# Reordering the weight conversion and the products of the first two chunk indices in a linear-attention and feed-forward kernel

## The chip, the cores and the metric

The kernel runs on one core of one Trainium2 chip. The metric is device time in microseconds (us) of one execution. TensorE does matrix products (PE in the profile, its weight loads PEld), VectorE (DVE) and ScalarE (ACT) do elementwise work, GpSimd (POOL) only fills constants here, and SyncE (SP) issues all DMAs in one queue. Each engine takes its instructions in the order in which they were built and waits for semaphores at the head of its queue.

## The reference: what is computed

For 4 batches, 8 heads, 768 time steps and 48 channels a linear-attention recurrence is computed, and its output, laid out as 3072 tokens by 384, goes through a multiplicative feed-forward block:

```python
for t in range(S):
    cur = einsum('bhd,bhe->bhde', u * k[t], v[t])
    y[t] = einsum('bhd,bhde->bhe', r[t], state + cur)
    state = w * state + einsum('bhd,bhe->bhde', k[t], v[t])
x = y.transpose(0, 2, 1, 3).reshape(3072, 384)
out = ((x @ w1) * (x @ w2)) @ w3 @ w_out     # 384 -> 1024 -> 1024 -> 384
```

The arrays r, k, v, w and u are float32. The feed-forward weights come as float64, and the kernel turns them into float32 itself.

## The kernel before, in words

**Units.** Time is cut into 6 chunks of 128 steps (the chunk index c), and a unit n is one chunk of one batch b: n = 4c + b, 24 units in all. The recurrence runs from chunk to chunk through the state st of each batch. For a unit the kernel does, in the names of the code:

- `load` (line 129): three DMAs of 192 KB, k and r into krin (3 buffers) and v into vnat (3 buffers).
- `scale` (306): VectorE multiplies k and r by powers of w into krs (2 buffers), line 310.
- `diagonal` (314): VectorE forms r*k*u and its sums dg (lines 319 to 321), and ScalarE puts them on the diagonal of AT with eight activations (line 326).
- `turn` (337), for units 0 to 4: TensorE transposes k and r (line 342), and ScalarE copies them out (line 344) as kT and tt. From unit 5 on the transposition goes through VectorE (line 352), a DMA to a scratch in DRAM (354), four DMAs back (362) and a ScalarE copy (367).
- `pairs` (370): TensorE's k-v products (389) and r-k products (395) into PSUM; VectorE updates st (403, 408, 409); ScalarE spreads st into wide (420); VectorE puts the masked r-k products over the diagonal in AT (416).
- `output` (455): TensorE's products of the state (473) and of AT with v (483); ScalarE copies the sum into xT, the feed-forward input of the chunk (488).

**Feed-forward.** For each chunk index, x @ w1 and x @ w2 are made in 8 column blocks j of 128: `ab(c, j)` (line 493) computes three products of 128x512 into ps_a, a ScalarE copy (502), three into ps_b, and a VectorE multiplication (506) into abt. A block can be done for half of the tokens (batches 0 and 1, or 2 and 3): then the products have 256 columns. The profile counts every such float32 product as two matmuls. w3 and w_out are multiplied once into a 1024x384 matrix (`fold`, 290), and `sums` and `o` (524, 534) finish the output.

**Weights.** w1 and w2 are cut in strips of 256 columns: piece 2z is strip z of w1, piece 2z + 1 is strip z of w2, 8 pieces in all, 768 KB each. `fetch` (147) asks for the float64 words of a piece into one of three raw buffers. `convert` (254) makes float32 of them: ScalarE line 266, VectorE lines 267, 268 and 269, ScalarE line 271, VectorE line 272. Block j needs strip j // 2 of both matrices. Pieces 0 and 1 are fetched before the program branches (165, 170); a piece whose raw buffer is still in use waits on SyncE, and everything behind it in SyncE's queue waits too.

**Order of the work.** The order is written out by hand in `beside` (586): for every chunk index a list of 8 slots, two to a unit; the first is done ahead of the unit's output, the second behind the next unit's pairs. From index 2 on the slots are cut from one merged list. The loop (606 to 636) takes, for unit n: loads, scale, diagonal and turn of unit n + 1, slot 2b, output of n, pairs of n + 1, slot 2b + 1. The instruction streams that are built follow this order only roughly, since the tool that builds the program places instructions by its own priorities; where the text speaks of the built order, the streams of the finished programs were read.

Of the kernel before, what the change touches and what calls it, by code (L numbers as in the profile page):

```python
# [21 lines left out]
def kernel(  # L22
# [35 lines left out]
    B, H, S, D = r.shape  # L58
# [8 lines left out]
    DF = moe_w3.shape[0]  # L67
    KM = DM // P
    KF = DF // P
# [3 lines left out]
    STRIP = 256  # L73
# [7 lines left out]
    def rows(i):  # L81
        return slice(i * PAD, (i + 1) * PAD)
# [46 lines left out]
    def load(n, which="krv"):  # L129
        if n >= NU:  # L130
            return
        c, b = units[n]
        ts = slice(c * C, (c + 1) * C)
        for nm, src, dst in (("k", k, krin[n % NIN][:, 0]), ("r", r, krin[n % NIN][:, 1]), ("v", v, vnat[n % NV][:, :, :D])):
            if nm in which:
                nc.sync.dma_start(out=dst, in_=src[b, :, ts, :].rearrange("h t d -> t h d"))
# [10 lines left out]
    def fetch(piece):  # L147

        dst, src = piece
        if src.dtype != U64:  # L150
            nc.sync.dma_start(out=dst, in_=src)
            return None
        _, m, n = src.shape
        raw = raws[sent[0] % NRAW][:, :m * n].rearrange("p (m n) -> p m n", m=m)
        sent[0] += 1
        nc.sync.dma_start(out=raw, in_=src)
        return raw
# [25 lines left out]
    with tc.tile_pool(name="once", bufs=1) as once, tc.tile_pool(name="psW", bufs=2, space=PSUM) as psW:  # L183
# [12 lines left out]
        for l in range(LEVELS):  # L196
            n = 1 << l
# [20 lines left out]
    def body(arm, fast):  # L218
# [13 lines left out]
        else:  # L232
# [6 lines left out]
            for l in range(LEVELS):  # L239
                n = 1 << l  # L240
# [13 lines left out]
        def convert(piece, raw):  # L254
            dst, src = piece
            if src.dtype != U64:
                return
            _, m, n = src.shape
            lo, hi = (raw.bitcast(U32).rearrange("p m (n z) -> p m n z", z=2)[:, :, :, z] for z in range(2))
            t, power = (once.tile([P, RAW], F32, tag="cv", bufs=3 if fast else 2, name=nm)[:, :m * n].rearrange("p (m n) -> p m n", m=m)  # L260
                        for nm in ("t", "power"))
            tb, hb, pb = t.bitcast(U32), dst.bitcast(U32), power.bitcast(U32)

            nc.scalar.activation(out=power, in_=hi.bitcast(F32), func=ABS)  # L266
            nc.vector.tensor_scalar_max(power, power, 2.0 ** -15)  # L267
            nc.vector.tensor_scalar(tb, hi, 0x80000000, None, ALU.bitwise_and)
            nc.vector.scalar_tensor_tensor(hb, pb, 3, tb, ALU.logical_shift_left, ALU.bitwise_xor)  # L269

            nc.scalar.activation(out=t, in_=lo, func=IDENTITY, bias=two, scale=2.0 ** -51)  # L271
            nc.vector.tensor_add(hb, hb, tb)
# [33 lines left out]
        def scale(n):  # L306

            kr = krin[n % NIN]
            if fast:
                nc.vector.tensor_mul(krs[n % NS][:, :, :, :D], kr, pn[:, :, :, :D])  # L310
            else:
                nc.scalar.copy(out=krs[n % NS][:, :, :, :D], in_=kr)
# [142 lines left out]
        def output(n):  # L455
            c, b = units[n]
            rw = rT[n]
            if not fast:
                rw = work.tile([P, NP, C], F32, tag="kl", bufs=1, name=f"rw{n}")
                for p in range(NP):  # L460
                    nc.gpsimd.tensor_mul(rw[:, p].rearrange("x (a t) -> x a t", a=2),
                                         rT[n][:, p].rearrange("x (a t) -> x a t", a=2),
                                         pw[:, p, None, :].to_broadcast([P, 2, T]))
            yt = psY.tile([P, 2, 512], F32, tag="y", name=f"ps_y{n}")
            ps = yt[:, :, :KM * T].rearrange("x a (q t) -> x a q t", q=KM)


            blocks = [(p, j, divmod(3 * p + j, P // Q)) for p in range(NP) for j in range(3)]
            to = lambda a, q, g: ps[g * Q:(g + 1) * Q, a, q, :]
            held = range(0 if c else 1, 2)  # L470
            for a in held:
                for p, j, (q, g) in blocks:
                    nc.tensor.matmul(to(a, q, g), lhsT=wide[a][n % 2][:, p, j * Q:(j + 1) * Q], rhs=rw[:, p, 2 * a:2 * a + 2] if fast else rw[:, p, rows(a)],  # L473
                                     start=(q == 0), stop=False, skip_group_check=True)

            vv = vnat[n % NV].rearrange("t h d -> t (h d)")
            parts = [(h, f) for h in range(H) for f in range(h * D // PAD, ((h + 1) * D - 1) // PAD + 1)]
            seen = set()
            for h, f in sorted(parts, key=lambda e: (e[0] * D > e[1] * PAD, e[1])):
                x = h * PD + f * PAD - h * D  # L480
                q, g = divmod(f, 2)
                for a in range(2):
                    nc.tensor.matmul(ps[rows(g), a, q, :], lhsT=vv[rows(a), x:x + PAD], rhs=AT[n][rows(a), h % 2, h // 2, :],  # L483
                                     start=(a not in held and (a, g) not in seen), stop=True, skip_group_check=True)
                    seen.add((a, g))
            if b == 0:
                xT[c] = work.tile([P, KM, NT], F32, tag="xT", bufs=2, name=f"xT{c}")
            nc.scalar.copy(out=xT[c][:, :, b * C:(b + 1) * C].rearrange("x q (a t) -> x a q t", a=2), in_=ps)  # L488
# [70 lines left out]
        def AB(c, js=range(KF), ts=slice(0, NT)):  # L559
            return [lambda c=c, j=j: ab(c, j, ts) for j in js]  # L560

        def O(c):
            return [lambda c=c, j=j: sums(c, j) for j in range(KH)] + [lambda c=c, m=m: o(c, m) for m in range(B // 2)]

        def first(i):
            if i not in landed:
                landed[i] = fetch(ab_pieces[i])
            convert(ab_pieces[i], landed[i])

        W12 = [[lambda i=i: first(i) for i in (2 * z, 2 * z + 1)] for z in range(DF // STRIP)]  # L570
        WO = [lambda c=c: out_weight(c) for c in range(KF)]

        def W3(js):
            return [s for j in js for s in ([lambda j=j, z=z: w3_weight(j, z) for z in range(DF // PIECE)]
                                            + [lambda j=j: fold(j)])]

        def merge(*lists):

            keyed = [((i + 0.5) / len(x), m, s) for m, x in enumerate(lists) for i, s in enumerate(x)]
            return [s for _, _, s in sorted(keyed, key=lambda e: e[:2])]  # L580
# [3 lines left out]
        halves = [slice(0, NT // 2), slice(NT // 2, NT)]  # L584
        none = []
        beside = [
            [none, none, none, W12[0] + AB(0, range(0, 2), halves[0]), none, W12[1][:1], none,
             AB(0, range(0, 2), halves[1]) + W12[1][1:] + AB(0, range(2, 4))],
            [none, W12[2], none, AB(0, range(4, 6)), none, W12[3], none, AB(0, range(6, 8))],
            merge(AB(1), WO + W3(range(3))),  # L590
            merge(AB(2, range(1)), W3(range(3, KF))) + [sums_of_weights] + merge(AB(2, range(1, lead)), O(0)[:KH])
            + O(0)[KH:] + AB(2, range(lead, KF)),
            O(1) + merge(O(2), AB(3)),
# [4 lines left out]
        before = dict(landed)  # L598

        free = B + 1 if fast else NU + 1  # L600
        scale(0)
        diagonal(0)
        turn(0)
# [2 lines left out]
        for c in range(NCH):  # L606
            plan = beside[c]
            if not isinstance(plan[0], list):
                cuts = [len(plan) * m // (2 * B) for m in range(2 * B + 1)]
                plan = [plan[cuts[m]:cuts[m + 1]] for m in range(2 * B)]  # L610
            for b in range(B):
                n = c * B + b
                while asked <= (n + 3 if n + 3 >= free else n + 2):
                    load(asked, "kr")
                    asked += 1
                load(n + 2, "v")
                if n + 1 < min(NU, free):
                    scale(n + 1)
                if n + 1 < NU:
                    diagonal(n + 1)  # L620
                    if n + 1 >= free:
                        turn_rows(n + 1)
                if n + 1 < min(NU, free):
                    turn(n + 1)
                if free <= n + 2 < NU:
                    scale(n + 2)
                    turn_blocks(n + 2)
                for step in plan[2 * b]:
                    step()
                output(n)  # L630
                if free <= n + 2 < NU:
                    turn_places(n + 2)
                if n + 1 < NU:
                    pairs(n + 1)
                for step in plan[2 * b + 1]:
                    step()
        for step in tail:
            step()
        landed.clear()
# [38 lines left out]
```

## Time and profile before

| what | value |
|---|---|
| median of 5 runs | 526.21 us (525.19 to 526.72) |
| the profiled execution's own time | 527.77 us |
| its span, first to last instruction | 525.8 us |
| mean granted TensorE clock | 0.986 |
| TensorE busy | 496.1 us |
| VectorE busy | 281.5 us |
| ScalarE busy | 195.5 us |
| HBM read, written | 39.65 MB, 12.19 MB |
| TensorE busy in 20 to 40, 40 to 60 us | 17.62, 14.99 us |
| VectorE busy in 20 to 40, 40 to 60 us | 18.04, 18.97 us |
| TensorE busy in 300 to 400 us | 100.00 us |

How to read it: the page gives one profiled execution. Its slices are fortieths of the span, some 13.1 us each, with the busy share in tenths. In a timeline line the numbers are the start and the length, then engine, line of the code, operation, tiles, shapes and the count of instructions; in brackets stands the idle time ahead of the group and what ended it. Start to start, neighbouring instructions of one engine lie closer than their lengths, because they overlap at their ends.

### The profile page before, as it was taken

How to read it: one execution, taken by the hardware profiler on the slowest of the kernel's cores; microseconds unless marked ns; L12 is line 12 of the kernel's file. 1: busy time of each engine (PE TensorE's matmuls, PEld its weight loads, DVE VectorE, ACT ScalarE, POOL GpSimd, SP SyncE). 2: the span in 40 equal slices, each digit the busy share in tenths (PEclk: the TensorE clock that was granted, in tenths of full speed). 3: DMA queues.
4: the chain of work that ended last, by engine and by line, in shares of the span. 5: the costliest groups of instructions: out<-in, count | busy, mean ns of one | idle time of the engine just before them, and what ended most of it. 6: DMA issues, size and time to landing. Idle time of an engine off the chain costs nothing.

```text
span 525.8 us, 12272 instructions
## 1 busy us (share of the span) xinstructions
PE 496.1 (94%) x5192; PEld 324.8 (62%) x5192; DVE 281.5 (54%) x616; ACT 195.5 (37%) x487; POOL 6.0 (1%) x23
## 2 busy tenths in 40 slices
PE   2697999999999999999999999999999999999996
PEld 2586454555555656659746975497555777954486
DVE  5889888669864675492642464324531216211442
ACT  3888376556754666430133114212143110001000
POOL 4000000000000000000000000000000000000000
PEclk9878999999999999999999999999999999999999
DMA  7988756748686463240130414112021000000001
GB/s 186 235 215 223 198 133 155 186 147 197 168 255 152 150 181 99 65 106 32 41 97 23 115 57 107 50 42 65 31 76 32 1 32 31 32 30 1 0 0 67
DMA packets 96867, 52.73 MB, mean 100 GB/s; under 512 B 77730, under 2 KB 88227, under 8 KB 96803
## 3 DMA queue, kind: packets, MB, share of 16 engines
q1 hardware_dynamic: 96802, 51.86, 36.5%
q8 instruction: 43, 0.70, 0.6%
q14 instruction: 22, 0.17, 0.1%
HBM read 39.65 MB, written 12.19 MB: 99 GB/s over the span
## 4 chain that ended last, share of the span: by engine, by line
PE 83%; DVE 7%; DMA 4%; ACT 3%; issue 2%; SPq 0%; DVEq 0%; ACTq 0%
PE ps_b L505 22%; PE ps_a L500 22%; PE ps_w L300 8%; PE ps_y L483 3%; PE ps_y L473 3%; PE ps_s3t L539 3%; PE ps_s4b L539 3%; PE ps_s1t L539 3%; PE ps_a22t L539 3%; PE ps_a12b L539 3%; PE ps_s2t L539 3%; PE ps_a11b L539 3%; DMA krin<-in_r_dram 2%; PE ps_a L395 2%; DMA raw<-in_moe_w_dram 2%
## 5 line engine op out<-in xcount | busy, mean ns | idle before, releaser
L505 PE MATMUL ps_b<-xT,w 128*128 128x512 f32 (+1 forms) x300 | 133.1, 578 | 1.4 <-ACT a L502 1.2
L500 PE MATMUL ps_a<-xT,w 128*128 128x512 f32 (+1 forms) x300 | 134.3, 584 | 0.0
L505 PEld LDWEIGHTS ps_b<-xT,w 128*128 128x128 f32 x300 | 56.2, 190 | 67.0 <-issue 59.5
L506 DVE TENSOR_TENSOR abt<-ps_b,a 128x512 f32<-128x512 f32 (+1 forms) x50 | 33.4, 668 | 117.2 <-PE ps_b L505 116.9
L500 PEld LDWEIGHTS ps_a<-xT,w 128*128 128x128 f32 x300 | 55.7, 192 | 58.5 <-issue 53.0
L502 ACT COPY a<-ps_a 128x512 f32<-128x512 f32 (+1 forms) x50 | 28.4, 567 | 148.5 <-PE ps_a L500 148.1
L326 ACT ACTIVATE AT<-same,dg 128x64 f32<-128x64 f32 x192 | 48.8, 336 | 0.3
L420 ACT COPY wide<-st 64x192 f32<-64x192 f32 x88 | 30.7, 349 | 43.4 <-PE ps_y L473 27.0
L300 PE MATMUL ps_w<-wo,w3T 128*128 128x384 f32 x128 | 43.1, 490 | 2.3 <-ACT w3T L297 2.3
L300 PEld LDWEIGHTS ps_w<-wo,w3T 128*128 128x128 f32 x128 | 23.7, 190 | 17.9 <-ACT w3T L297 2.8
L473 PEld LDWEIGHTS ps_y<-tt,wide 128*32 128x32 f32 x1056 | 18.5, 112 | 24.8 <-issue 17.5
L310 DVE TENSOR_TENSOR krs<-krin,pn_in 128x768 f32<-128x768 f32 x24 | 22.9, 955 | 19.6 <-PE ps_a L389 10.1
L473 PE MATMUL ps_y<-tt,wide 128*32 128x64 f32 x1056 | 25.4, 226 | 7.4 <-ACT wide L420 3.9
L271 ACT ACTIVATE t<-raw,two 128x512 f32<-128x512 uint32 (+2 forms) x32 | 25.5, 803 | 10.2 <-DVE wo L269 5.5
L266 ACT ACTIVATE power<-raw 128x512 f32<-128x512 f32 (+2 forms) x32 | 22.3, 704 | 14.3 <-DMA raw<-in_moe_w_dram 13.7
L483 PE MATMUL ps_y<-AT,vnat 64*64 64x64 f32 x1152 | 24.3, 233 | 1.5 <-DVE AT L416 1.5
L483 PEld LDWEIGHTS ps_y<-AT,vnat 64*64 64x64 f32 x1152 | 20.8, 144 | 6.3 <-DVE AT L416 1.9
L545 ACT COPY m<-ps_a11b 128x192 f32<-128x192 f32 x12 | 3.8, 318 | 53.5 <-PE ps_a11b L539 53.5
L267 DVE TENSOR_SCALAR power<-power 128x512 f32<-128x512 f32 (+2 forms) x32 | 14.0, 437 | 10.6 <-ACT power L266 10.5
L395 PE MATMUL ps_a<-tt,kT 64*64 64x64 f32 x768 | 18.8, 234 | 0.7 <-issue 0.7
L488 ACT COPY xT<-ps_y 128x384 f32<-128x384 f32 x24 | 11.4, 474 | 21.6 <-PE ps_y L483 15.8
L352 DVE STREAM_TRANSPOSE tr<-krs 128x768 f32<-128x768 f32 x19 | 18.5, 975 | 0.5
(92 smaller groups left out, 582.5 us busy)
## 6 DMA issues: line engine op xcount, KB each, us to landing
raw<-in_moe_w_dram SPq DMA_DIRECT2D x16, 512.0 KB, 4.7
scratch<-tr SPq DMA_DIRECT2D x19, 384.0 KB, 3.2
raw<-in_moe_w_dram SPq DMA_DIRECT2D x8, 768.0 KB, 6.0
tt<-scratch SPq DMA_DIRECT2D x38, 128.0 KB, 2.9
krin<-in_k_dram SPq DMA_DIRECT2D x24, 192.0 KB, 4.1
krin<-in_r_dram SPq DMA_DIRECT2D x24, 192.0 KB, 4.3
vnat<-in_v_dram SPq DMA_DIRECT2D x24, 192.0 KB, 3.5
out_dram<-osb SPq DMA_DIRECT2D x24, 192.0 KB, 1.9
```

Source lines behind the costliest of these rows:

```text
L271: nc.scalar.activation(out=t, in_=lo, func=IDENTITY, bias=two, scale=2.0 ** -51)
L300: nc.tensor.matmul(ps, lhsT=w3T[:, kc, :], rhs=wo[kc], start=(kc == 0), stop=(kc == KF - 1))
L326: nc.scalar.activation(out=AT[n][:, i, p, :], in_=same, func=COPY, scale=dg[:, h:h + 1])
L395: nc.tensor.matmul(ps[rows(a), i, p, :], lhsT=kT[n][rows(i), p, rows(a)], rhs=rT[n][rows(i), p, 2 * a:2 * a + 2], start=True, stop=True)
L420: nc.scalar.copy(out=wide[a][n % 2][rows(i), :, i * D:(i + 1) * D], in_=st[units[n][1]][rows(i)])
L473: nc.tensor.matmul(to(a, q, g), lhsT=wide[a][n % 2][:, p, j * Q:(j + 1) * Q], rhs=rw[:, p, 2 * a:2 * a + 2] if fast else rw[:, p, rows(a)] ...
L483: nc.tensor.matmul(ps[rows(g), a, q, :], lhsT=vv[rows(a), x:x + PAD], rhs=AT[n][rows(a), h % 2, h // 2, :], start=(a not in held and (a, g ...
L500: nc.tensor.matmul(pa[:, :n], lhsT=w1[:, z, q, js], rhs=xT[c][:, q, ts], start=(q == 0), stop=(q == KM - 1))
L502: nc.scalar.copy(out=a[:, :n], in_=pa[:, :n])
L505: nc.tensor.matmul(pb[:, :n], lhsT=w2[:, z, q, js], rhs=xT[c][:, q, ts], start=(q == 0), stop=(q == KM - 1))
L506: nc.vector.tensor_mul(abt[c, j][:, ts], pb[:, :n], a[:, :n])
L539: nc.tensor.matmul(ps, lhsT=made[c, j][a][:, m * C:(m + 1) * C], rhs=made[b][:, j, :], start=(j == 0), stop=(j == KH - 1))
```

## The change

Piece 0 is converted ahead of unit 0. The other pieces get new slots: pieces 1 to 4 in index 0 and pieces 5 to 7 in index 1. Pieces that were converted in pairs stand alone. A new function `early` fetches a piece without converting it, and is called at the end of the loop for the first three units. At unit 3 the output and the slot stand ahead of unit 4's scale, and the output ahead of the slot; at other units the order is as it was. Blocks 4 to 7 of chunk 0 come one or two units earlier, and blocks 0 to 3 of chunk 1 are cut in halves of 256 columns, the first halves in index 1, the second in index 2.

```diff
+        def early(i):
             if i not in landed:
                 landed[i] = fetch(ab_pieces[i])
+
+        def first(i):
+            early(i)
             convert(ab_pieces[i], landed[i])
 
-        W12 = [[lambda i=i: first(i) for i in (2 * z, 2 * z + 1)] for z in range(DF // STRIP)]
+        def W12(*pieces):
+            return [lambda i=i: first(i) for i in pieces]
+
...
         beside = [
-            [none, none, none, W12[0] + AB(0, range(0, 2), halves[0]), none, W12[1][:1], none,
-             AB(0, range(0, 2), halves[1]) + W12[1][1:] + AB(0, range(2, 4))],
-            [none, W12[2], none, AB(0, range(4, 6)), none, W12[3], none, AB(0, range(6, 8))],
-            merge(AB(1), WO + W3(range(3))),
+            [none, W12(1), none, none, AB(0, range(0, 2), halves[0]), W12(2),
+             AB(0, range(0, 2), halves[1]) + W12(3), AB(0, range(2, 4)) + W12(4)],
+            [W12(5), AB(0, range(4, 6)) + W12(6), W12(7), AB(0, range(6, 8)),
+             none, AB(1, range(0, 2), halves[0]), none, AB(1, range(2, 4), halves[0])],
+            merge(AB(1, range(0, 4), halves[1]) + AB(1, range(4, KF)), WO + W3(range(3))),
...
+        first(0)
         scale(0)
         diagonal(0)
...
                 load(n + 2, "v")
+                if n + 1 == B:
+                    output(n)
+                    for step in plan[2 * b]:
+                        step()
                 if n + 1 < min(NU, free):
                     scale(n + 1)
...
-                for step in plan[2 * b]:
-                    step()
-                output(n)
+                if n + 1 != B:
+                    for step in plan[2 * b]:
+                        step()
+                    output(n)
...
                 for step in plan[2 * b + 1]:
                     step()
+                if n + 1 < B:
+                    early(n + 2)
```

More of the change, by code (lines that the diff above doesn't have):

```diff
@@ L563, in O @@
             return [lambda c=c, j=j: sums(c, j) for j in range(KH)] + [lambda c=c, m=m: o(c, m) for m in range(B // 2)]
-        def first(i):
+        def early(i):
             if i not in landed:
                 landed[i] = fetch(ab_pieces[i])
+        def first(i):
+            early(i)
             convert(ab_pieces[i], landed[i])
-        W12 = [[lambda i=i: first(i) for i in (2 * z, 2 * z + 1)] for z in range(DF // STRIP)]
+        def W12(*pieces):
+            return [lambda i=i: first(i) for i in pieces]
         WO = [lambda c=c: out_weight(c) for c in range(KF)]
```

## The prediction

> **What bounds the kernel now.** I read the page's busy shares and slices first, then the waits, then the sum by windows, then TensorE's, ScalarE's and VectorE's timelines up to 100 us, and last the built order of instructions of both kernels.
>
> ```profile
> PE 496.1 (94%) x5192; PEld 324.8 (62%) x5192; DVE 281.5 (54%) x616; ACT 195.5 (37%) x487; POOL 6.0 (1%) x23
> ...
> PE   2697999999999999999999999999999999999996
> ...
> DVE  5889888669864675492642464324531216211442
> ...
> PEclk9878999999999999999999999999999999999999
> DMA  7988756748686463240130414112021000000001
> ```
>
> TensorE is busy 94% of the span. From about 57 us on it hardly stops; its idle time and its lowered clock are in the first five slices, and there VectorE and the DMA engines are full. So the change can win only what TensorE loses before some 90 us, and lose by making that longer.
>
> ```profile
> 20.00:25.00 5.00, 4.41 (x140) 3.63 (x139) 5.00 (x11) 4.95 (x16) 0.00 (x0) 0.70 0.92 239
> 25.00:30.00 5.00, 3.20 (x54) 2.56 (x58) 4.74 (x9) 4.93 (x14) 0.00 (x0) 0.64 0.90 227
> 30.00:35.00 5.00, 5.00 (x110) 4.58 (x104) 4.16 (x8) 3.09 (x10) 0.00 (x0) 0.67 0.80 175
> ...
> 45.00:50.00 5.00, 3.66 (x135) 3.38 (x125) 5.00 (x10) 3.63 (x11) 0.00 (x0) 0.69 0.99 268
> ```
>
> Columns: TensorE, weight load, VectorE, ScalarE, GpSimd busy; granted clock; DMA share; GB/s. VectorE is busy 5.00 of 5.00 where TensorE is not. TensorE's timeline names the gaps:
>
> ```profile
> 26.80 1.18 PE L473 MATMUL ps_y<-tt,wide 128*32 128x64 f32 x24 [2.21 <-issue]
> ...
> 44.42 0.91 PE L473 MATMUL ps_y<-tt,wide 128*32 128x64 f32 x24 [2.38 <-ACT wide L420]
> 46.66 1.39 PE L483 MATMUL ps_y<-AT,vnat 64*64 64x64 f32 x48 [1.34 <-DVE AT L416]
> ...
> 55.82 1.56 PE L505 MATMUL ps_b<-xT,w 128*128 128x256 f32 x6 [1.22 <-ACT a L502]
> ```
>
> and further on 0.92 us at 74.48 (waiting for wide, L420) and 1.01 us at 89.24.
>
> **Part 1, the head: piece 0 ahead of unit 0.** Conversion of a 768-column piece is, start to start on VectorE, 0.47 (L267) + 0.47 (L268) + 0.87 (L269) + 0.87 (L272) = 2.68 us, and 0.8 to 0.9 (L266) + 0.9 to 1.0 (L271) on ScalarE. The sum of this work is unchanged; its place is not. In the built order ScalarE now has piece 1's L266 ahead of unit 0's copies L344. Before they ran at 12.51 and 13.32; piece 1 was used as soon as it landed:
>
> ```profile
> 15.19 0.90 ACT L266 ACTIVATE power<-raw 128x768 f32<-128x768 f32 x1 [1.29 <-DMA raw<-in_moe_w_dram]
> ```
>
> So these copies now wait behind the landing: ScalarE is held from 11.2 to 15.2, L266 ends at 16.1, the copies at 17.1 (+3.2 us). TensorE's L395 of unit 0 goes from 14.1 to 17.15. What hides it: before, VectorE waited at the head of its queue too, 2.08 us for unit 2's r until 17.47, and took unit 0's st (L403) only at 18.81. Now unit 2's scale stands later; VectorE reaches piece 0's L272 at 18.1 (after ScalarE's L271), L403 at 18.97. Then ScalarE's two L420 end at 20.6, L416 at 21.54, and unit 0's L483 starts at 21.6, against 21.45. Without that cover the head would cost the 3.2 us. Value taken: +0.15.
>
> **Part 2, the DMA queue.** Piece 2 (768 KB) is now asked for ahead of unit 3's k and r. 3264 KB (k, r of units 0 to 2, v of 0 and 1, u, pieces 0 and 1) went from the issue at 2.08 to the landing at 17.34: 214 KB per us. Then v of unit 2, piece 2 and unit 3's k and r, 1344 KB, take 6.3 us: 23.6. VectorE wants unit 3 at 24.5, so 0.9 us spare. Piece 2 lands at 21.8, wanted at 21.6, with 0.7 us of cover (the dg it is ahead of is ready at 22.3). If transfers overlap, unit 3 could come as late as piece 3: 27.2, 2.7 us late. I take in order: 0.
> The Trainium skill, "DMA: Bandwidth & Descriptors", section "Queues, rings and completion order", says that each DMA engine starts a queue's descriptors in ring order; this speaks against putting a piece ahead of a unit, and by it unit 3 waits for all of piece 2, which is the 0 taken here. No row of this trace separates two transfers of the queue.
>
> **Part 3, to the first strip.** VectorE's order up to unit 3's st (L403) now holds piece 3's L272 and piece 4's L268 and L269 more, and unit 5's L319 and L320 less: +0.87 +0.47 +0.87 -0.94 = +1.27. Its idle time from 10.23 was 4.5 us; placing each instruction behind its waits I find 3.4 now (0.85 for piece 1's L266, 1.06 for piece 0's L271, 0.47 for unit 0's L420, 0.65 for piece 2's L271, the rest in steps of 0.05 to 0.2). So L403 of unit 3 comes at 43.8 against 43.63. On the way the first xT half is complete at 32.2, and the first a, b product starts at 32.4 against 32.58. Unit 3's L483 starts at 46.35 against 46.66. That the output of unit 3 and its products now stand ahead of unit 4's scale in the source moves nothing here: the built order still has unit 4's L310 and transposes ahead of that output. So the early chain is a draw within 1 us each way: the same chain of VectorE, ScalarE and TensorE sets it.
>
> **Part 4, 46 to 68 us.** Before, 46.66 to the start of j=2 at 57.22 took 10.56 us, in it 0.4 of unit 4's L473 and the 1.22 gap: ScalarE's a-copy stood behind an L266 that waited 1.55 us for a piece. Now that piece is asked for earlier. Piece 5 is issued at about 36.7 (after piece 2's L271) and with the page's 6.0 us to landing is there at 42.7, wanted at 43.1. Piece 6, issued at 40.2, with the longest landing of a piece in this stretch (8.8) is there at 49.0, wanted at 48.1; TensorE has about 1 us in hand there (the a-copy frees at 51.2 what it needs at 51.3). So 46.35 + 10.56 - 0.4 - 1.22 = 55.3, a lead of 57.22 - 55.3 - 0.4 = **1.5 us**; bounds: -2 (gap remains and pieces land late) to +3.
>
> **Part 5, units 4 to 7.** Before, only one product lay between pairs (L389, L395) of unit 5 and its output, and TensorE waited 0.17 + 0.92, and 1.01 at unit 6. Now two whole j, 4 x 2.58 = 10.3 us, lie there; from pairs to L416 VectorE needs about 5.2 us (L310 0.87, L352 0.9, L408, L409, L416 and what stands between). All of **2.1 us** go. For units 7 and 9 only four half products, 5.2 us and an L473 of 0.8, lie between; L416 comes 4.8 us after the pairs. No wait, with 1.2 us spare. The pieces are ready: strips 2 and 3 end at 53.9 and 65, wanted at 68 and 81. VectorE's own load between pairs of 7 and 8 is 7.9 us for 7.8 us of TensorE, so this spare is thin; bounds 0 to 2.1.
>
> **Part 6, halves.** Four j of chunk 1 are cut in two: 8 products of 512 columns (2.58 us) become 16 of 256. Their step was 1.29 twice and 1.40 twice where the clock was high, mean 1.34: 8 x (2 x 1.34 - 2.58) = **+0.9 us**; bounds 0 (1.29) and 1.8 (1.40). Four more copies on ScalarE and four more multiplications on VectorE, under 0.3 us each in sum, lie beside TensorE. Between pairs of unit 5 and the first fold TensorE has the same products in both orders, so the folds come no earlier against their weights.
>
> **Sum**, on the profiled execution's 527.77 (span 525.8 and 1.97 around it): 527.77 - 1.5 - 2.1 + 0.9 = 525.1. It was 1.56 above the median of the runs, 526.21; on that scale **523.5 us**.
>
> **The clock.** The sum lets it be as before, since the gaps at 25 and 43 us stay. After the 2.38 us gap the clock granted in 45:50 was 0.69, and L483's 48 matmuls took 1.39 against 0.93 at 86 us. If both gaps vanished, the slowed stretches (0.64 to 0.70 over 20 us) would give back up to 0.33 x 20 = 6.6 us.
> The Trainium skill, "TensorE: Matmul & The Clock Gate", section "HAM oscillation — how this bites in real kernels", wants gaps over about 3.4 us before the clock halves; the row at 45:50 shows it lowered after gaps of 2.38 and 1.34. By that rule the longer head gap of part 1 (14.2 to 17.1) would cost no clock and neither would the others, so nothing could be won there; by the row shorter gaps matter, both ways.
>
> **Rivals.**
> - *Slower: the weights go ahead of the units.* Place: ScalarE's queue, where piece 5's L266 stands ahead of unit 4's kT copy and of unit 3's L420, and the DMA queue, where piece 2 stands ahead of unit 3. If piece 5 takes 8.8 us, as piece 6 did before, it lands at 45.5, 2.4 us behind the 43.1 at which ScalarE wants it; unit 3 landing at 27.2 adds 2.7 us less little. 523.5 + 2.4 + 2.7 = 528.6 with the clock as it is. It decides for slower once such slips sum to 3.8 us. For it: DMA share 0.8 to 1.06 up to 60 us, and L266 waiting for pieces three times before. Against: each piece now has one more unit's time to land. Chance 0.25.
> - *No change.* VectorE is the true bound: the gaps of parts 4 and 5 come back at units 7 and 9, where VectorE has 7.9 us of work in 7.8. 527.77 + 0.9 - 1 = 527.7, or 526.1 on the median's scale. Chance 0.12.
> - *Much faster.* The gaps at 25 and 43 us shrink and the clock stays up: half of the 6.6 us more, 520.2. Against: VectorE's order reaches L403 of unit 3 no sooner. Chance 0.13.
> - Forecast, 522 to 525: 0.50.
>
> **How the numbers follow.** 0.2% of 526.2 is 1.05 us, about what a measurement can tell. Faster by more: 0.50 + 0.13 = 0.63; within: 0.12; slower: 0.25. The range goes from 519.8 (most of the third rival) to 528.0 (the greater part of the first), leaving some 0.2 out.
>
> **What would show it.** Right: ScalarE idle from about 11 to 15 us before L266; unit 0's L483 at about 21.6; the first 256-column product near 32.4; no 1.22 us wait before L505 near 54; j=2 starting near 55; no wait of TensorE between 65 and 100; 48 more records of the 256-column form and 24 fewer of the 512-column form, for L500 and for L505 each. Wrong: L266 waiting for raw over 1 us between 20 and 50, L310 waiting for krin after 20 us, or new L473 waits at units 7 and 9.

## The result, and the profile after

The changed kernel took 528.18 us (median of 38 runs, 526.59 to 529.96) against 526.4 us (75 runs, 524.56 to 529.36): ratio 1.0037, 95% interval [1.003, 1.0044]. So it is **slower** by 0.37%, 1.8 us, where 523.5 us and faster were forecast, and 0.2 us outside the range.

The gaps that the change was to close did close behind 60 us, and yet the time rose. The 1.8 us fall in two parts. Of each run, the span and what lies around it are known: the median span of after is 525.45 us, and 2.85 us lie around it (2.69 to 3.19 in 40 runs). Before has 2.0 around (1.93 to 2.08 in one set of 35), a span of about 526.4 - 2.0 = 524.4. So **0.85 us of the loss lie outside the span and about 1.0 us inside**. The profiled execution of after is 529.03 us with a span of 526.2.

The page of after, TensorE, VectorE, granted clock and DMA in 40 slices:

```profile
PE 496.7 (94%) x5240; PEld 333.2 (63%) x5240; DVE 282.9 (54%) x620; ACT 195.3 (37%) x491; POOL 6.0 (1%) x23
...
PE   2687999999999999999999999999999999999996
...
DVE  6889898868664675493643464324531216211442
...
PEclk9987999999999999999999999999999999999999
DMA  7978667666665463340131314212021000000001
```

TensorE's busy time is the same within 0.6 us, and its idle slices are still the first four. The head, in ScalarE's timeline and then in TensorE's:

```profile
15.68 0.89 ACT L266 ACTIVATE power<-raw 128x768 f32<-128x768 f32 x1 [4.53 <-DMA raw<-in_moe_w_dram]
16.47 0.57 ACT L344 COPY kT<-ps_kT 128x512 f32<-128x512 f32 x1
```

```profile
17.58 1.14 PE L395 MATMUL ps_a<-tt,kT 64*64 64x64 f32 x32 [3.27 <-ACT tt L344]
...
27.91 0.55 PE L342 MATMUL ps_kT<-ident,krs 128*128 128x128 f32 x3 [2.29 <-DVE w L272]
...
33.45 1.56 PE L500 MATMUL ps_a<-xT,w 128*128 128x256 f32 x6
...
45.56 0.92 PE L473 MATMUL ps_y<-tt,wide 128*32 128x64 f32 x24 [2.79 <-ACT wide L420]
47.15 1.56 PE L483 MATMUL ps_y<-AT,vnat 64*64 64x64 f32 x48 [0.68 <-DVE AT L416]
...
49.31 2.93 PE L500 MATMUL ps_a<-xT,w 128*128 128x256 f32 x6
52.03 2.02 PE L505 MATMUL ps_b<-xT,w 128*128 128x256 f32 x6
53.89 1.46 PE L500 MATMUL ps_a<-xT,w 128*128 128x256 f32 x6
...
57.41 2.84 PE L500 MATMUL ps_a<-xT,w 128*128 128x512 f32 x6
```

The same products before:

```profile
49.69 1.86 PE L500 MATMUL ps_a<-xT,w 128*128 128x256 f32 x6
51.39 1.46 PE L505 MATMUL ps_b<-xT,w 128*128 128x256 f32 x6
...
57.22 2.74 PE L500 MATMUL ps_a<-xT,w 128*128 128x512 f32 x6
```

ScalarE is held by piece 1 and both long gaps are still there (2.29 and 2.79 us, against 2.21 and 2.38). The second halves of blocks 0 and 1 start at 49.31 and their first product takes 2.72 us to the next where 1.70 was seen before: the clock granted in 45 to 50 us is 0.63, and 0.68 in 50 to 55 (before: 0.69 and 0.97). j = 2 starts at 57.41, against 57.22. Further on, TensorE's groups that waited:

```profile
101.36 1.56 PE L500 MATMUL ps_a<-xT,w 128*128 128x256 f32 x6 [0.64 <-ACT a L502]
...
123.90 1.56 PE L505 MATMUL ps_b<-xT,w 128*128 128x256 f32 x6 [0.92 <-DVE abt L506]
...
139.66 0.34 PE L395 MATMUL ps_a<-tt,kT 64*64 64x64 f32 x7 [0.96 <-issue]
```

From 60 to 100 us the waits of 0.92 and 1.01 us are gone. What that is worth is read from three marks of after and, below them, three of before:

```profile
84.25 2.84 PE L500 MATMUL ps_a<-xT,w 128*128 128x512 f32 x6
...
97.86 1.56 PE L500 MATMUL ps_a<-xT,w 128*128 128x256 f32 x6
...
137.62 0.63 PE L389 MATMUL ps_a<-vnat,krs 64*64 64x48 f32 x32
```

```profile
85.27 0.88 PE L473 MATMUL ps_y<-tt,wide 128*32 128x64 f32 x48
...
103.24 2.74 PE L500 MATMUL ps_a<-xT,w 128*128 128x512 f32 x6
...
136.88 0.63 PE L389 MATMUL ps_a<-vnat,krs 64*64 64x48 f32 x32
```

At the end of block 5 (84.25, against 85.27) TensorE has done the same work in both, 1.0 us earlier in after. Chunk 1's products start at 97.86, against 103.24; before has done one output and one set of pairs more by then, 2.6 us where they stand alone, so after leads by some 2.8 us. At the pairs of unit 11, again with equal work, it is 0.7 us behind (137.62, against 136.88). So the stage with the halves takes some 3.5 us more than before's blocks (the same marks in e9 and e17 against e18, further executions of the two orders, give 3.5 too), and only 1.56 of them are the waits of 0.64 and 0.92; the rest lies in the shorter products and in groups of L473 that are cut in two.

### The profile page after: what moved, and what is told of

It reads as the page before. It is cut to its first block, busy times and chain, and to the rows that moved or that the text cites. A ratio compares the mean times of both kernels' runs of the same rounds, so it can differ in the third digit from the quotient of the medians.

```text
span 526.2 us, 12388 instructions
## 1 busy us (share of the span) xinstructions
PE 496.7 (94%) x5240; PEld 333.2 (63%) x5240; DVE 282.9 (54%) x620; ACT 195.3 (37%) x491; POOL 6.0 (1%) x23
## 4 chain that ended last, share of the span: by engine, by line
PE 79%; DVE 7%; ACT 7%; DMA 3%; issue 2%; SPq 1%; ACTq 0%; DVEq 0%
PE ps_b L505 21%; PE ps_a L500 21%; PE ps_w L300 7%; PE ps_a12b L539 3%; PE ps_s3t L539 3%; PE ps_y L483 3%; PE ps_s4b L539 3%; PE ps_a22t L539 3%; PE ps_s2t L539 3%; PE ps_s1t L539 3%; ACT AT L326 3%; PE ps_y L473 3%; PE ps_a11b L539 3%; DMA raw<-in_moe_w_dram 2%; PE ps_a L395 1%
## 5 line engine op out<-in xcount | busy, mean ns | idle before, releaser
L500 PE MATMUL ps_a<-xT,w 128*128 128x512 f32 (+1 forms) x324 | 136.3, 557 | 1.2 <-ACT a L502 1.2
L505 PEld LDWEIGHTS ps_b<-xT,w 128*128 128x128 f32 x324 | 61.6, 192 | 65.1 <-issue 56.9
L500 PEld LDWEIGHTS ps_a<-xT,w 128*128 128x128 f32 x324 | 60.0, 192 | 56.6 <-issue 47.5
L506 DVE TENSOR_TENSOR abt<-ps_b,a 128x512 f32<-128x512 f32 (+1 forms) x54 | 34.0, 630 | 114.6 <-PE ps_b L505 114.4
L502 ACT COPY a<-ps_a 128x512 f32<-128x512 f32 (+1 forms) x54 | 28.9, 536 | 149.5 <-PE ps_a L500 139.2
L310 DVE TENSOR_TENSOR krs<-krin,pn_in 128x768 f32<-128x768 f32 x24 | 22.9, 955 | 16.1 <-PE ps_a L389 10.3
L473 PEld LDWEIGHTS ps_y<-tt,wide 128*32 128x32 f32 x1056 | 18.0, 111 | 19.3 <-issue 13.4
L266 ACT ACTIVATE power<-raw 128x512 f32<-128x512 f32 (+2 forms) x32 | 22.4, 703 | 14.0 <-DMA raw<-in_moe_w_dram 12.1
L473 PE MATMUL ps_y<-tt,wide 128*32 128x64 f32 x1056 | 24.6, 224 | 2.9 <-ACT wide L420 2.8
L483 PE MATMUL ps_y<-AT,vnat 64*64 64x64 f32 x1152 | 24.0, 231 | 0.8 <-DVE AT L416 0.8
L395 PE MATMUL ps_a<-tt,kT 64*64 64x64 f32 x768 | 18.5, 226 | 5.3 <-ACT tt L344 3.3
L483 PEld LDWEIGHTS ps_y<-AT,vnat 64*64 64x64 f32 x1152 | 20.5, 143 | 4.3 <-DVE AT L416 1.3
L395 PEld LDWEIGHTS ps_a<-tt,kT 64*64 64x64 f32 x768 | 15.7, 138 | 5.8 <-ACT tt L344 3.4
```

Source lines behind the costliest of these rows:

```text
L395: nc.tensor.matmul(ps[rows(a), i, p, :], lhsT=kT[n][rows(i), p, rows(a)], rhs=rT[n][rows(i), p, 2 * a:2 * a + 2], start=True, stop=True)
L500: nc.tensor.matmul(pa[:, :n], lhsT=w1[:, z, q, js], rhs=xT[c][:, q, ts], start=(q == 0), stop=(q == KM - 1))
L502: nc.scalar.copy(out=a[:, :n], in_=pa[:, :n])
L505: nc.tensor.matmul(pb[:, :n], lhsT=w2[:, z, q, js], rhs=xT[c][:, q, ts], start=(q == 0), stop=(q == KM - 1))
L506: nc.vector.tensor_mul(abt[c, j][:, ts], pb[:, :n], a[:, :n])
```

## The experiments

All were timed in five rounds beside the kernel before on the same chip. In the table, "span" is the median span minus that of before in the same set of runs, in us, with a 95% interval from resampling the runs; "around" is the median of time minus span, where before has 1.85 to 2.01.

| kernel | ratio to before, 95% interval | span | around |
|---|---|---|---|
| e1 head alone | 1.0002 [0.9987, 1.0017] | 0.0 [-0.4, 0.4] | 2.16 |
| e2 after without the head | 1.0056 [1.0028, 1.0084] | +3.8 [2.0, 5.1] | 1.43 |
| e3 index 1 with halves alone | 0.9999 [0.9985, 1.0014] | -0.65 [-1.05, -0.1] | 2.69 |
| e4 after, piece 1 fetched first | 1.0033 [1.0017, 1.0048] | +1.7 [1.2, 2.4] | 2.78 |
| e5 head and index 1 | 1.0031 [1.0019, 1.0043] | +0.6 [-0.1, 1.1] | 2.98 |
| e6 rest of index 0 alone | 1.0016 [1.0002, 1.0031] | +0.45 [-0.3, 1.5] | 1.72 |
| e7 after without early fetches | 1.0028 [1.0016, 1.004] | +1.45 [0.9, 2.4] | 1.75 |
| e8 after without the swap at unit 3 | 1.0019 [1.0009, 1.0029] | +0.65 [-0.1, 1.05] | 2.77 |
| e9 before, halves in the arm not run | 1.0015 [0.9999, 1.0031] | +0.4 [-0.1, 0.9] | 2.11 |
| e10 after, none in the arm not run | 1.004 [1.0026, 1.0053] | +1.4 [1.0, 2.15] | 2.73 |
| e11 after without halves | 1.0081 [1.0057, 1.0104] | +3.4 [2.5, 4.45] | 2.61 |
| e12 index 1 alone, no halves | 1.0054 [1.0036, 1.0071] | +1.8 [1.2, 3.0] | 2.67 |
| e17 before with idle copies | 1.0016 [1.0004, 1.0027] | +0.3 [-0.1, 1.0] | 2.83 |
| e18 after with idle copies | 1.0009 [0.9997, 1.002] | +0.5 [-0.1, 1.4] | 1.76 |

### Which part of the change loses it: e1 to e4

e1 adds to the kernel before:

```diff
+        first(0)
         scale(0)
...
-            [none, none, none, W12[0] + AB(0, range(0, 2), halves[0]), none, W12[1][:1], none,
+            [none, W12[0][1:], none, AB(0, range(0, 2), halves[0]), none, W12[1][:1], none,
```

> The kernel before, with piece 0 converted ahead of unit 0 and piece 1 in the second slot, and nothing else of the change. Theory H (the head: ScalarE's queue is held behind piece 1's landing, and the early chain comes 1 us later and meets a lowered clock): 0.8 to 1.5 us slower than before, ScalarE idle about 4.5 us before the second L266. Theory X (the halved products of chunk 1 lose it, at 97 to 140 us): within 0.5 us of before.

The head alone costs nothing, 0.0 us. ScalarE was held as in after: L395 of unit 0 started at 17.09 after a gap of 2.77 us, and the first half product all the same at 32.19.

e2 takes the same two edits out of after (`W12(0, 1)` in slot 3 instead).

> The changed kernel with the head as before: pieces 0 and 1 converted in the fourth slot. Theory H: 1 to 1.5 us faster than the changed kernel, about 526.9. Theory X: as the changed kernel, 528.2, with TensorE's waits of 0.64 and 0.92 us between 97 and 125 us still there.

Worse than after: without its head the rest is 3.8 us longer in span than before, with runs from 524.5 to 532.0. So the head isn't what makes after slow.

e3 changes the kernel before in the second and third lists alone:

```diff
-            [none, W12[2], none, AB(0, range(4, 6)), none, W12[3], none, AB(0, range(6, 8))],
-            merge(AB(1), WO + W3(range(3))),
+            [W12[2][1:], AB(0, range(4, 6)) + W12[3][:1], W12[3][1:], AB(0, range(6, 8)),
+             none, AB(1, range(0, 2), halves[0]), none, AB(1, range(2, 4), halves[0])],
+            merge(AB(1, range(0, 4), halves[1]) + AB(1, range(4, KF)), WO + W3(range(3))),
```

(and piece 4 into the last slot of index 0).

> The kernel before with the change's second index (strips 2 and 3 one or two units earlier, blocks 4 to 7 earlier, blocks 0 to 3 of chunk 1 halved), head and loop as before. Theory X: 1 to 2 us slower than before, with waits of TensorE between 97 and 140 us of 2 us or more. Theory H: 0 to 1.5 us faster than before, since the gaps of 2.1 us at units 5 and 6 go.

The part that was forecast to gain does gain: 0.65 us of span. The same kernel has 0.7 us more around it, and the total is even.

e4 fetches piece 1 ahead of v of unit 0 and k, r of unit 1:

```diff
+    landed[1] = fetch(ab_pieces[1])
     load(0, "v")
     load(1, "kr")
-    landed[1] = fetch(ab_pieces[1])
```

> The changed kernel with piece 1 asked for ahead of v of unit 0 and of unit 1, so that ScalarE's L266 of piece 1 doesn't wait. Theory H: the copies L344 of unit 0 move from 16.5 to about 13, and the kernel is 0.5 to 1.5 us faster than the changed one. Theory X: as the changed kernel, 528.2 within 0.4.

No gain: as after, though the copies L344 came at 13.76 as expected.

### Parts of the change together: e5 to e8

e5 is e1's and e3's edits together.

> The kernel before with both the change's head and its second index, without the rest of the change in the first index (the early fetch, the output of unit 3 ahead of unit 4's scale, the slots of pieces 2 to 4). Theory F (the first index's other edits lose it): at most as slow as before, 524 to 526. Theory X' (head and halves together lose it): 527 to 528.

Alone they give 0.0 and -0.65 us of span, together +0.6 [-0.1, 1.1]. The two don't add up, but the 1.25 us between them are hardly more than the widths of the three intervals, and no single profile shows a place for it. Theory F's 524 to 526 us was missed (528.35); the 527 to 528 of X' was nearer, but 1.0 us of the loss lies around the span.

e6 is after with e2's edit, and with the second and third lists as before (only piece 5 a slot earlier), so it has the early fetches, the swap at unit 3 and the slots of pieces 2 to 4 alone.

> Only those other edits of the first index: early fetch, unit 3's output ahead of unit 4's scale, slots of pieces 2 to 4; head, second index and whole blocks as before. Theory F: 1.5 to 3 us slower than before, j=2 starting at 57 us or later. Theory X': as before within 0.5.

e7 and e8 take single parts out of after:

```diff
-                if n + 1 < B:
-                    early(n + 2)
```

```diff
-                if n + 1 == B:
-                    output(n)
-                    for step in plan[2 * b]:
-                        step()
...
-                if n + 1 != B:
-                    for step in plan[2 * b]:
-                        step()
-                    output(n)
+                for step in plan[2 * b]:
+                    step()
+                output(n)
```

(in e8 the second halves of blocks 0 and 1 stand one slot later).

> The changed kernel without the early fetch of pieces 2 to 4. If piece 2 ahead of unit 3 in the DMA queue is the loss: 1 to 2 us faster than the changed kernel (526 to 527), unit 3's scale sooner. If it is the order at unit 3: as the changed kernel, 528.2 within 0.4.

> The changed kernel with unit 3's output at its old place behind unit 4's scale and turn, and the second halves of blocks 0 and 1 in the slot after it. If the order at unit 3 is the loss: 1 to 2 us faster than the changed kernel (526 to 527). If it is the early fetch: as the changed kernel, 528.2 within 0.4.

e6 is only 0.45 us longer in span (Theory F expected 1.5 to 3 in all), and neither e7 nor e8 gets back to before's total. But e7 doesn't clear the early fetches. Its last computation, in its profile and in that of after:

```profile
520.26 0.36 DVE L553 TENSOR_TENSOR osb<-ps_s4b,u 128x192 f32<-128x192 f32 x1 [0.68 <-PE ps_s4b L539]
```

```profile
522.31 0.36 DVE L553 TENSOR_TENSOR osb<-ps_s4b,u 128x192 f32<-128x192 f32 x1 [0.68 <-PE ps_s4b L539]
```

Both profiled spans are 526.2 us. That of e7 runs on for 5.58 us behind its last computation, that of after for 3.53; 14 of the 16 profiles of full length have 3.53 to 3.87 there, and besides e7 only e2 stands out, with 4.96. Less this end, the computation of e7 ends in the median some 0.5 us ahead of that of before in the same set (526.3 - 5.58, against 524.85 - 3.6), and that of e8 0.6 us behind it: estimates that take each program's end from one profile. So a longer end may hide in e7 what the early fetches cost, and 1.4 of e2's 3.8 us may lie in the end too.

### The halves: e11 and e12

e11 is after, e12 the kernel before with e3's earlier strips and blocks 4 to 7, both with blocks 0 to 3 of chunk 1 whole in the third list:

```diff
-             none, AB(1, range(0, 2), halves[0]), none, AB(1, range(2, 4), halves[0])],
-            merge(AB(1, range(0, 4), halves[1]) + AB(1, range(4, KF)), WO + W3(range(3))),
+             none, none, none, none],
+            merge(AB(1), WO + W3(range(3))),
```

> The changed kernel with blocks 0 to 3 of the second index whole again, in the third index's list as before. Both T and W: the instructions are about 12272 again, the end is 5.4 to 5.9 us and the time around the span about 2.0. TensorE's waits of 0.64 and 0.92 us in 100 to 140 us vanish. Theory X' (halves with the head lose it): span 1 us below that of after, total 526.3 (ratio 0.9995 to 1.0005). Rival Y (the index 0 part and the clock's phase lose it, whatever the halves): span as after, ratio 1.002.

> The kernel before with piece 4 in the last slot of the first index and pieces 5 to 7 and blocks 4 to 7 of the second index one slot earlier; no halves, nothing else of the change. If the earlier strips and blocks are worth the 1.0 us that the trace of after shows at the end of block row 5, and the halves alone give it back: span 1 us below before, time around the span 2.0, ratio 0.998. If the gaps only move behind the units: ratio 1.000.

Both expectations were wrong, and by much: without the halves both kernels are slower. TensorE of e12 behind the pairs of unit 7, and the same stretch by windows (columns as in the prediction; 0.77 and 0.55 are the granted clock):

```profile
94.06 0.71 PE L395 MATMUL ps_a<-tt,kT 64*64 64x64 f32 x32
94.97 0.54 PE L473 MATMUL ps_y<-tt,wide 128*32 128x64 f32 x24 [0.19 <-ACT xT L488]
99.00 1.23 PE L473 MATMUL ps_y<-tt,wide 128*32 128x64 f32 x24 [3.49 <-ACT wide L420]
```

```profile
95.00:100.00 5.00, 1.51 (x48) 1.15 (x48) 4.97 (x11) 4.86 (x15) 0.00 (x0) 0.77 0.67 173
100.00:105.00 5.00, 4.78 (x124) 3.77 (x115) 4.50 (x9) 2.90 (x10) 0.00 (x0) 0.55 0.39 78
```

And e3, which differs by the halves alone:

```profile
94.03 0.71 PE L395 MATMUL ps_a<-tt,kT 64*64 64x64 f32 x32
94.67 1.56 PE L500 MATMUL ps_a<-xT,w 128*128 128x256 f32 x6
...
98.19 1.56 PE L500 MATMUL ps_a<-xT,w 128*128 128x256 f32 x6 [0.66 <-ACT a L502]
```

Both reach L395 of unit 7 at the same time (94.06 and 94.03). The chain through VectorE and ScalarE to unit 7's wide takes 4.9 us; with the halves TensorE has products in it, without them it stands for 3.49 us, and the clock falls to 0.55. So the halves are worth 1.8 + 0.65 = 2.4 us of span, 525.5 against 523.05, and the waits of 0.64 and 0.92 us in after are part of their price. The earlier blocks only move the gaps behind units that then have no products: the halves are what fills them.

### Where in the span: e13 to e16

The executed arm is cut off behind the first (e13, e14) or the third index (e15, e16); everything later, with the outputs, is left out:

```diff
-        for c in range(NCH):
+        for c in range(1 if fast else NCH):
...
-        for step in tail:
+        for step in [] if fast else tail:
```

(in e14 piece 4 isn't converted, so that both convert the same four pieces, but it is fetched, which e13 doesn't do.)

> The kernel before, cut off behind the first index: it leaves out the second to sixth index, the fold and all outputs. Its span's median is the level for e14; by the trace of before about 70 us.

> The changed kernel, cut off at the same place (outputs and all later work left out; of piece 4 the fetch is kept and the conversion left out, so that the same pieces are converted as in e13). The prediction's parts 1 to 4: span 1.4 us below e13. Theory S (the head's order starves the first index in most executions and the profiled execution of before was a slow draw): span equal to or 0.5 to 1.5 us above e13. Rival Y (all is lost in the second and third index): 0.5 to 1 us below e13.

> The kernel before, cut off behind the third index (the fourth to sixth index and all outputs left out). Its span's median is the level for e16, about 200 us.

> The changed kernel, cut off at the same place, with the same work done. If the span's loss lies in the first three indices: e16 minus e15 is 0.8 to 1.4 us. Theory S: that of e14 minus e13 or up to 0.5 us less. Rival Y: 0.5 to 1 us slower with e14 faster than e13. If e16 equals e15 or is faster, the loss lies behind the third index, where the change moves nothing, or only in the program as a whole.

Medians of all runs of each (five or six), spans:

| cut behind | before | after | difference, 95% interval |
|---|---|---|---|
| index 0 | 67.05 (65.8 to 67.9) | 69.3 (68.1 to 70.8) | +2.25 [1.3, 3.5] |
| index 2 | 178.9 (177.9 to 180.0) | 180.45 (179.4 to 182.3) | +1.55 [-0.1, 3.4] |

With only the runs within 1.5% of the fastest of each kernel (2, 3, 5 and 4) the differences are +2.45 and +0.7 us. The second row is not clear of noise, so the rows don't show what the later two indices do. The first is not the size in the whole kernel: piece 4's 768 KB are fetched in e14 and not in e13, and later work that both kernels have in full is missing from both. In 45 to 50 us VectorE is busy 2.35 us in e13 and 0.32 in e14, the DMA share is 0.35 and 0.29; the kernel before has 5.00 us and 0.99 there.

The profiles of full length give the same place with a smaller size. From the start of j = 2 to the end of the span the order of before takes 468.6, 468.2 and 468.5 us (before, e9, e17), that of after 468.8, 468.55 and 468.5 (after, e10, e18). So what differs between executions of one order lies almost all ahead of j = 2. Taken off the median spans, 524.4 and 525.45, the means put j = 2 at 56.0 and 56.85, an estimate. So theory S has the place right: **the first index loses, some 0.85 us**, or 1.25 with the 0.4 us of unit 4's L473 that only before has done by then. Its reason, the head, isn't shown (0.0 us in e1).

### The time outside the span: e9, e10, e17, e18

e9 and e10 change only the arm that isn't executed (w outside its bounds): e9 gives it the halves on the kernel before, e10 takes them from it in after:

```diff
-             none, AB(1, range(0, 2), halves[0]), none, AB(1, range(2, 4), halves[0])],
+             none, AB(1, range(0, 2), halves[0]) if fast else none, none, AB(1, range(2, 4), halves[0]) if fast else none],
```

> The kernel before, with four half products per block row added in the second arm (w outside its bounds) alone, which isn't executed; the executed arm is that of before. Theory T (the time behind the last computation follows the program's size or layout, not the work executed): time around the span 2.7 to 3.0 us in place of 2.0, from the last VectorE operation to the device's end 6.3 to 7.3 us in place of 5.6; total 0.7 to 1 us over before (ratio 1.0013 to 1.002), span unchanged. Rival W (executed instructions make it): everything as before, ratio 1.000 and 2.0 us around.

> The changed kernel, with the halves kept out of the second arm, which isn't executed; the executed arm is that of after. Theory T: time around the span falls from 2.85 to about 2.0, total 527.3 (ratio 1.002). Rival W: 2.85 around as after, ratio 1.0037.

Nothing moved (2.11 and 2.73): the size of the arm that isn't run doesn't set it. e11 and e12 refute the other idea, that the halves' 116 more instructions do: with 12280 and 12276 instructions, against 12272 before, they have 2.61 and 2.67 around them. e17 and e18 put 24 copies of one element between the last pair products and the last output block, where TensorE bounds:

```diff
+        def pad():
+            padding = work.tile([1, 3, 8], F32, tag="pad", bufs=1, name="pad")
+            late = abt[NCH - 1, KF - 1]
+            for y in range(8):
+                nc.vector.tensor_copy(out=padding[:, 0, y:y + 1], in_=late[0:1, y:y + 1])
+                nc.scalar.copy(out=padding[:, 1, y:y + 1], in_=late[0:1, y:y + 1])
+                nc.gpsimd.tensor_copy(out=padding[:, 2, y:y + 1], in_=late[0:1, y:y + 1])
-        tail = O(4) + AB(5) + O(5)
+        tail = O(4) + AB(5) + ([pad] if fast else none) + O(5)
```

> The kernel before with 24 one-element copies (8 each on VectorE, ScalarE and GpSimd) between the last pair products and the last output block, where TensorE bounds: they do nothing for the result. Theory T2 (the time outside the span follows the program's layout): it moves by 0.3 us or more from 2.0, up or down, the span staying within 0.5 us. Rival W2 (it follows the order of the second index's work): 1.9 to 2.2 us as before.

> The changed kernel with the same 24 copies. Theory T2: the time outside the span moves by 0.3 us or more from 2.85, most likely down, as there is more room below. Rival W2: 2.7 to 3.0 us as after.

The time around moved as T2 expected: the same idle copies bring before from 1.85 to 2.83 us around its span, and after from 2.85 to 1.76. The spans are +0.3 and +0.5 of that set's before. With the copies in both, the medians have after (526.86) 0.9 us ahead of before (527.80, interval of the difference -1.5 to +0.1, so not clear of noise); without them it is 1.8 us behind. So the 0.85 us around the span aren't tied to the change: copies that do nothing take them away from after and give them to before. What in the built program sets them isn't shown. Inside the span, after's order loses 0.5 us here [-0.1, 1.4] and 1.4 in e10 [1.0, 2.15]; its loss isn't known more closely than that.

## Why the prediction was wrong, step by step

- **Part 1, the head:** right in mechanism and size. ScalarE's wait, L483 of unit 0 at 22.02 (forecast 21.6) and e1's 0.0 us agree with +0.15.
- **Part 2, the DMA order:** nearly as forecast. Piece 2's L266 waited 0.50 us at 22.54 for its landing, the other four in 20 to 50 us not at all, and L310 for no krin.
- **Part 3, to the first strip:** mis-sized. L403 of unit 3 came at 44.53 (forecast 43.8), the first half product at 33.45 (32.4) and L483 of unit 3 at 47.15 (46.35): 0.7 to 1 us late in this execution. How much of it is typical the next point tells.
- **Part 4, the lead of 1.5 us: this step failed.** It was read as the difference from one execution, that of before, which began j = 2 at 57.22 after a 1.22 us gap and was 1.56 us above the median. By the estimate from the full profiles the median execution of before begins j = 2 at 56.0 and that of after at 56.85: 0.85 us later, or 1.25 with unit 4's L473 counted as the forecast did, where 1.5 us of gain were forecast. Five profiled executions of the order that before has in index 0 start j = 2 at 53.20 (e13), 54.04 (e15), 56.10 (e9), 57.22 (before) and 57.73 (e17); six of after's at 53.65 (e14), 54.60 (e11), 55.19 (e16), 57.34 (e18), 57.35 (e10) and 57.41 (after). The 1.22 us gap shows in before's profile alone, but its absence is no gain by itself: from L483 of unit 3 to j = 2 before takes 10.56 us with it, e9 and e17 take 10.63 and 10.53 without it, at clocks of 0.50 and 0.63 in 45 to 50 us, and after, also without it, takes 10.26 at 0.63. In e15 the same stretch reads

```profile
50.72 1.46 PE L500 MATMUL ps_a<-xT,w 128*128 128x256 f32 x6
52.10 0.52 PE L473 MATMUL ps_y<-tt,wide 128*32 128x64 f32 x18
52.64 1.56 PE L505 MATMUL ps_b<-xT,w 128*128 128x256 f32 x6
54.04 2.74 PE L500 MATMUL ps_a<-xT,w 128*128 128x512 f32 x6
```

  with unit 4's L473 between the products and j = 2 at 54.04, 3.2 us before the execution that I took for the rule. The sum removed 1.5 us against an execution that was by the estimate 1.2 us late at j = 2, and then took off its 1.56 us above the median as well: bad luck counted twice.
- **Part 5, units 4 to 7:** right in mechanism, mis-sized. The gaps of 0.92 and 1.01 us are gone and units 7 and 9 don't wait for L473. At equal work TensorE goes from 0.6 us behind at j = 2 (57.41, against 57.22 with the 0.4 us of L473) to some 2.8 us ahead at 97.86: 3.4 us gained where 2.1 were forecast (3.1 against e17, 2.7 against e9).
- **Part 6, the halves: the second step that failed, by its size.** Their stage costs some 3.5 us, where +0.9 was forecast (0.8 with the 1.34 us as printed) and at most 1.8. 1.56 of it are the waits of 0.64 and 0.92 us, with a cause not foreseen: the copies (L502, L506) stand in the queues of ScalarE and VectorE behind bursts. What I had not priced either is that Part 5 holds only with the halves; e12 does without, and loses 2.4 us against e3. Parts 5 and 6 together, -1.2 us forecast, measured -0.65 [-1.05, -0.1] in e3; in after, from j = 2 to the end of the span, 468.6 us against 468.4 before, nothing is gained (0.2 us with the 0.4 of unit 4's L473 counted).
- **Around the span:** the forecast left it at 1.97; it was 2.85, +0.85 us that no step spoke of.
- **The clock:** it stays low after the two gaps, as the sum took it, but varies between executions of one order: granted in 45 to 50 us 0.69 (before), 0.50 (e9), 0.71 (e15), 0.63 (e17), and 1.00 in the shortest, e13. In after, executions with a mean of 0.997 have spans of 523.8 to 525.1, those with 0.989 to 0.990 of 524.4 to 527.1. The Trainium skill, "TensorE: Matmul & The Clock Gate", section "HAM oscillation — how this bites in real kernels", has the clock halve after gaps over about 3.4 us; e12's 3.49 us agrees with that, the 0.63 after 2.79 and 0.68 us in after doesn't.

As sums: forecast -1.5 (first index), -1.2 (units and halves), 0 (around). Measured, with unit 4's L473 counted as the forecast did: +1.25 (the estimate at j = 2), -0.2 (behind it) and +0.85 (around), 1.9 us against 1.8 of the whole kernel. The slower rival had the place right, the first 57 us, but not the mechanism: no piece came late enough. **What stays open** is which instruction makes the first index longer. The head alone costs 0.0 us (e1). The early fetches, the swap and the slots together cost +0.45 [-0.3, 1.5] (e6), which leaves room for the 0.85, and e7 with its longer end doesn't clear the early fetches; taking out the swap brings back nothing clear of noise (e8). Profiles of single executions scatter by up to 4.5 us at j = 2 and can't show it. What in the program's layout sets the time around the span is open too. A kernel of e3's order with the shorter time around it could be some 0.65 us ahead of before; it wasn't tried, and none of those measured is faster than before.

## What to carry to other kernels

Before subtracting a gap that one profile shows, ask whether the median holds it: profile the same order more than once, and where a start-up stage scatters by several us, time the kernel cut off behind it. Time that lies outside the span belongs to the program as built, can move by 1 us either way with instructions that do nothing, and should be taken off before an order is judged; so should the end of the span behind the last computation, where it differs. Work that is pulled forward leaves a hole where it stood: count what fills TensorE's next wait before counting the gain, and price the filler by more than its own step.

## What the runs showed of the hardware that was not expected

- The time around the span is steady for a program (within 0.1 to 0.5 us in one set of runs) and differs between programs of nearly the same work: medians of 1.43 (e2), of 1.72 to 2.2 and of 2.6 to 3.0 us, and none between 2.2 and 2.6. 24 one-element copies moved it by +0.98 and by -1.09.
- From the end of the last VectorE instruction to the end of the span it is 3.53 to 3.87 us in 14 profiles of full length, 4.96 in e2 and 5.58 in e7.
- Eleven profiled executions, of both orders, reached j = 2 between 53.2 and 57.7 us; two of the same order differ by up to 4.5 us there (the earliest of each order is a kernel cut off behind index 0). From there to the end of the span six of full length differ by 0.6 us at most.
- The granted clock in 45 to 50 us lay between 0.50 and 0.71 in four executions of before's order of index 0, and was 1.00 in the fifth (e13). Behind gaps of 2.79 and 0.68 us it was 0.63 in after, behind 2.79 and 0.70 us 0.85 in e18.
